# Convolution stem, forward and backward: the last chunk of the first batch's input gradient multiplied in three products, one copy per seed, middle sums added at eviction

## The chip, the cores and the metric

The kernel runs on one core of a Trainium2 chip. The metric is the device time of one execution in microseconds (us), as the median of several runs. One further execution was taken with the hardware profiler; the views of the profile and of the trace come from it.

## The reference

A strided one-dimensional convolution, a group norm with one group per channel over time, a GELU, and the gradients of all of it. In short:

```python
B, T, D, K = 2, 16000, 256, 31          # all inputs bf16
s = 2; L = (T - K) // s + 1             # 7985
h = sum(einsum('blc,cd->bld', x[:, i:i + s*L:s, :], w[i]) for i in range(K))
mu  = h.sum(1) / L;  var = ((h - mu) ** 2).sum(1) / L
out = gelu((h - mu) / sqrt(var + 1e-5) * gn_gamma + gn_beta)     # tanh form
# outputs: out, and the gradients by x, w, gn_gamma, gn_beta for a given grad_out
```

## The kernel before

**Stages.** F0 and F1 are the forward convolution of batch 0 and 1, G0 and G1 the gradient by `x` (`input_grad`), W the gradient by `w` (`weight_grad`). The GELU and its derivative for batch 1 (`gelu_batch(1, ...)`, eight units of `gelu_unit`) run beside G0 on ACT and DVE. When all eight are done, `elem_finalize(1)` forms the sums of the group norm, and `e_load`/`e_comp` can then prepare the gradient of batch 1 for each chunk.

**Order.** No instruction stands where the Python code calls it. Each call of `add` records an operation with its engine, an estimated duration, and what it reads and writes; `Plan.order` gives each a due time (from the tensor engine's progress, a slack, and the tables `lead` and `fine`, whose keys are stage, function and caller) and lists the operations engine by engine. Each engine then runs its own list in order. Transfers above 4096 bytes are issued by SP (`load` at L548, transposes by `turn` at L553) in these stages, except the stores of the transposed gradient, which POOL issues.

**Input gradient.** For each of two batches the work is four chunks `c`, two halves `pr` of a chunk, and three branches `br` in the order B, A, C. Branches and leaves come from two nested three-product splittings: instead of multiplying two weight groups by two inputs four times, one multiplies sums and differences three times. For a branch there is a middle leaf B and two outer leaves A and C. The accumulators are two pairs of PSUM banks, `px` and `pt`. One branch and half goes so:

- `g_three_b` (4 matmuls) and `g_three_ac` (8) make the middle leaf, in three products itself, in `px`. An ACT copy (L1357) carries the common product over.
- `g_seed` puts the middle leaf into `pt` as well, so that both outer leaves start from it.
- `last(A)` and `last(C)`, called while the next branch is under way, add the outer leaves into `pt` and `px`, and `g_evac` empties them: branch B into the middle sums `GRB` (ACT, `keep`, L837), branches A and C into the result tile `HO`. There is one `HO`; its store to `out_1` is issued after leaf C of branch C.

**The outer leaves, two ways.** In batch 0 an outer leaf is `g_leaf`, 16 matmuls with 512 columns (leaf A of branch A has 4 of 256). The seed is one ACT copy, `keep`, and `g_evac` adds the middle sum on DVE (L1429). In batch 1 (`GO`, `GOC`) each outer leaf is split in three products too: `g_outer` (4 matmuls, for leaf A into bank 0 and for leaf C into bank 1 of `pt`) and `g_three_ac` (8), 12 instead of 16. That needs summed weights (`w2_outer`, six additions at L688 into `W2DO` and `W2DC`) and a further moving operand for each leaf (`third`, L1283, into `GUO` and `GUC`). The seed is then longer: each outer product is written twice into a buffer `GTB`, by an ACT copy of 2048 elements for branch B (L1393) or by a DVE add of 2048 which also adds the middle sums `GRB` for branches A and C (L1397, arena<-ps,arena), and a second DVE add (L1397, ps<-ps,arena) puts middle leaf plus `GTB` into both accumulators at once. Since the middle sums are in the seed, `g_evac` in batch 1 is a plain copy on ACT (`keep`, L837, bf16).

**Memory.** `GREG` names the 28,928 bytes in which the GELU of batch 1 has its six tiles and the transposed `grad_out`, in the order h (two), y, s, y2, z, grad_out; later tenants of these bytes wait until the GELU has read them. The 8,192 bytes after it, `DNO[True]`, hold the transposed gradients of chunks 0 to 2 of batch 0 on their way out.

The tables `lead` and `fine`, some 200 numbers, are left out here.

Of the kernel before, what the change touches and what calls it, by code (L numbers as in the profile page):

```python
# [38 lines left out]
class Plan:  # L39
# [3 lines left out]
    def __init__(self, tc):  # L43
# [10 lines left out]
            "F0 f_evac last": -14.0,  # L54
            "F0 f_mm f_leaf": -265.0,
            "F0 f_mm f_outer": -52.5,
            "F0 f_mm f_three_ac": 2.5,
            "F0 f_mm f_three_b": 14.5,
            "F0 f_mm pe_turn": -455.5,
            "F0 f_outer forward": -66.5,  # L60
            "F0 f_three_b forward": 4.0,
            "F0 tt f_sums": -93.5,
            "F0 tt second": 49.5,
            "F0 tt third": 3.5,
            "F0 turn w2_part": 60.5,
            "F0 turn x_load": -50.0,
            "F0 ve f_seed": -129.5,
            "F0 ve_neg f_seed": 32.5,
            "F0 w_sub f_first": -46.5,
            "F0 zero x_load": 114.0,  # L70
            "F1 f_evac last": -156.5,
            "F1 f_mm f_leaf": -458.5,
            "F1 f_mm f_outer": 2.0,
            "F1 f_mm f_three_ac": -9.0,
            "F1 f_mm f_three_b": -31.5,
            "F1 f_outer forward": 4.0,
            "F1 f_seed forward": -37.0,
            "F1 f_three_b forward": -63.5,
            "F1 gelu_batch conv_stem_kernel": 10.5,
            "F1 gelu_unit gelu_batch": -1.5,  # L80
            "F1 load f_evac": 80.5,
            "F1 load gelu_unit": 22.0,
            "F1 load out0_store": 26.0,
            "F1 tiny elem_finalize": -56.0,
            "F1 tiny fwd_stats": -32.5,
            "F1 tt f_sums": -80.5,
            "F1 tt gelu_unit": -62.5,
            "F1 tt second": -41.0,
            "F1 tt third": -90.0,
            "F1 turn gelu_batch": 40.0,  # L90
            "F1 turn gelu_unit": -25.0,
            "F1 turn x_load": 33.0,
            "F1 ve f_seed": 8.0,
            "F1 ve_neg f_seed": -111.0,
            "F1 w_sub f_again": 35.5,
            "F1 zero f_evac": -103.0,
            "G0 cp e_comp": -6.0,
            "G0 e_comp e_load": -0.5,
            "G0 g_evac last": -13.0,
            "G0 g_mm g_leaf": -8.5,  # L100
            "G0 g_mm g_three_b": -8.0,
            "G0 g_three_b input_grad": 0.5,
            "G0 gelu_unit gelu_batch": -2.0,
            "G0 keep g_evac": -59.0,
            "G0 keep g_seed": -46.5,
            "G0 load dl_turn": 8.5,
            "G0 load e_load": 38.0,
            "G0 load g_evac": 18.0,
            "G0 load gelu_unit": 2.0,
            "G0 load load_w2": -9.0,  # L110
            "G0 spread e_comp": -1.0,
            "G0 tiny elem_finalize": -9.5,
            "G0 tt first": -52.5,
            "G0 tt gelu_unit": -0.5,
            "G0 tt third": -15.0,
            "G0 turn dl_turn": 5.0,
            "G0 turn gelu_batch": 7.5,
            "G0 w_sum load_w2": 23.0,
            "G0 zero e_comp": 10.0,
            "G1 cp e_comp": -75.5,  # L120
            "G1 e_comp e_load": 13.0,
            "G1 g_evac last": -1.5,
            "G1 g_mm g_leaf": -94.0,
            "G1 g_mm g_outer": -5.5,
            "G1 g_mm g_three_ac": -9.0,
            "G1 g_mm g_three_b": -33.0,
            "G1 g_three_b input_grad": -10.5,
            "G1 keep g_evac": 3.5,
            "G1 load dl_turn": 11.0,
            "G1 load e_load": -7.0,  # L130
            "G1 load g_evac": 15.5,
            "G1 plus g_seed": 1.5,
            "G1 spread e_comp": -6.5,
            "G1 spread g_seed": -150.0,
            "G1 tt first": -16.0,
            "G1 tt second": -15.0,
            "G1 tt third": -54.5,
            "G1 turn dl_turn": 3.5,
            "G1 w_sum w2_outer": 27.5,
            "G1 zero e_comp": -8.5,  # L140
            "W keep w_keep": -34.5,
            "W keep weight_grad": 6.0,
            "W leaf_d weight_grad": -3.0,
            "W load d_tile": -37.5,
            "W load out0_late": 105.0,
            "W load w_emit": 11.0,
            "W load weight_grad": 41.5,
            "W load x_raw": 1.5,
            "W pair_d weight_grad": -7.0,
            "W pair_x weight_grad": 0.5,  # L150
            "W turn out0_late": -77.0,
            "W ve w_done": -20.0,
            "W ve weight_grad": -19.5,
            "W w_add weight_grad": 1.0,
            "W w_add x_tile": -4.0,
            "W w_both weight_grad": 10.0,
            "W w_emit w_done": -5.0,
            "W w_emit weight_grad": -389.5,
# [310 lines left out]
def conv_stem_kernel(  # L469
# [13 lines left out]
    nc = tc.nc  # L483
# [894 lines left out]

    def g_seed(br, px, pt, outer, both):

        vx, vt = px[:], pt[:]

        def twice(v, k):
            d = [list(x) for x in v.ap]
# [513 lines left out]
```

## Time and profile before

| | us |
|---|---|
| median of 3 runs | 1165.74 |
| lowest and highest | 1163.94, 1165.88 |
| the profiled execution | 1166.96 |
| its span, first to last instruction | 1165.2 |
| mean granted clock of the tensor engine | 0.995 |

In the page, "busy" of an engine is the time in which it executed, and the number behind the bar of a group is its idle time just before the group's instructions with what ended it. A line number is that of the helper that records the operation, so a group is told by its line, its shapes and its operands: L1330 are all matmuls of the input gradient, L742 those of the forward pass, L1565 those of the weight gradient. The profiler misses some matmul records (x1880 on L1330), but not the weight loads (x1920), so matmuls are counted by weight loads. PE stands for the tensor engine, DVE for the vector engine, ACT for the scalar engine.

### The profile page before, as it was taken

The numbers are of one execution on the slowest core, as the hardware profiler recorded it, in microseconds if no ns is written. First come the engines' busy times: TensorE is split into PE (matmuls) and PEld (weight loads), VectorE is DVE, ScalarE is ACT, GpSimd is POOL, SyncE is SP. The second block draws the span as 40 slices with busy tenths as digits, with TensorE's granted clock in tenths as the row PEclk, the third lists the DMA queues.
The fourth block names the chain that finished last, engine by engine and source line by source line (L and its number), as shares of the span: only waits on it lengthen the run. The fifth ranks groups of instructions, "written<-read, shape, count | busy, mean of one in ns | idle before, by whom it ended". The sixth has DMA issues, their size and how long they took to land. (4 is left out here: it accounts for less than half of the span.)

```text
span 1165.2 us, 18856 instructions
## 1 busy us (share of the span) xinstructions
PE 1128.7 (97%) x7645; PEld 753.8 (65%) x7700; DVE 982.8 (84%) x892; ACT 553.3 (47%) x833; POOL 134.8 (12%) x221
## 2 busy tenths in 40 slices
PE   5999999999999989999899999999999999999998
PEld 3888899867777864444344444444478756666785
DVE  7997687798989997989687768777799997799995
ACT  1244454677776478788654464664332202111200
POOL 0000000000000021243232242241200000000000
PEclk8999999999999999999999999999999999999999
DMA  9476748868896598999997887676999926899367
GB/s 217 62 182 128 173 140 146 188 142 183 202 225 162 195 366 228 221 301 233 251 252 196 184 213 147 166 193 175 219 331 242 294 94 216 284 352 340 120 209 187
DMA packets 345806, 243.56 MB, mean 209 GB/s; under 512 B 233377, under 2 KB 316967, under 8 KB 341543
## 3 DMA queue, kind: packets, MB, share of 16 engines
q1 hardware_dynamic: 338615, 223.47, 73.0%
q0 software_dynamic: 7104, 18.89, 5.8%
q8 instruction: 60, 0.98, 0.4%
q14 instruction: 27, 0.22, 0.1%
HBM read 106.24 MB, written 80.25 MB: 160 GB/s over the span
## 5 line engine op out<-in xcount | busy, mean ns | idle before, releaser
L1330 PE MATMUL ps<-arena 128*128 128x512 bf16 (+1 forms) x1880 | 412.1, 377 | 13.3 <-DVE arena L1429 2.8
L742 PE MATMUL ps<-arena 128*128 128x256 bf16 (+4 forms) x3460 | 408.8, 282 | 15.7 <-DMA arena<-in_x_dram 5.7
L742 PEld LDWEIGHTS <-arena 128*128 128x128 bf16 x3460 | 338.9, 99 | 85.6 <-issue 8.6
L1330 PEld LDWEIGHTS <-arena 128*128 128x128 bf16 x1920 | 188.2, 98 | 236.0 <-issue 16.9
L1565 PE MATMUL ps<-arena 128*128 128x256 bf16 (+1 forms) x2305 | 308.6, 296 | 3.6 <-DVE arena L1635 1.9
L1565 PEld LDWEIGHTS <-arena 128*128 128x128 bf16 x2320 | 226.7, 98 | 85.6 <-DVE arena L1635 3.0
L837 ACT ACTIVATE arena<-ps 128x1024 f32<-128x1024 f32 (+1 forms) x111 | 113.0, 1022 | 242.6 <-PE ps L1565 84.1
L700 DVE TENSOR_TENSOR arena<-arena 128x2080 bf16<-128x2080 bf16 (+7 forms) x126 | 156.5, 1265 | 26.1 <-PE ps L742 25.5
L548 POOL DMA_DIRECT2D dld<-arena x144 | 105.2, 732 | 291.6 <-DMA arena<-arena 283.8
L1117 DVE TENSOR_TENSOR arena<-arena 128x2048 bf16<-128x2048 bf16 (+1 forms) x80 | 95.6, 1195 | 11.5 <-ACT arena L1109 6.0
L1533 DVE TENSOR_TENSOR arena<-arena 128x4096 bf16<-128x4096 bf16 x38 | 86.5, 2284 | 6.2 <-DMA arena<-in_x_dram 5.7
L1283 DVE TENSOR_TENSOR arena<-arena 128x1032 bf16<-128x1032 bf16 (+1 forms) x120 | 84.1, 725 | 8.3 <-PE ps L1330 5.2
L1397 DVE TENSOR_TENSOR ps<-ps,arena 128x2048 f32<-128x2048 f32 x24 | 55.1, 2297 | 25.2 <-PE ps L1330 24.4
L857 ACT ACTIVATE arena<-ps 128x512 bf16<-128x512 f32 (+1 forms) x64 | 37.1, 581 | 52.0 <-PE ps L742 50.2
L557 POOL MEMSET arena<- 128x128 bf16 (+11 forms) x40 | 9.1, 260 | 409.2 <-DVE arena L700 142.4
L1667 ACT COPY ps<-ps 128x256 f32<-128x256 f32 x54 | 19.3, 358 | 75.3 <-PE ps L1565 73.6
L1429 DVE TENSOR_TENSOR arena<-ps,arena 128x1024 bf16<-128x1024 f32 x32 | 38.8, 1218 | 12.9 <-PE ps L1330 7.6
L1397 DVE TENSOR_TENSOR arena<-ps,arena 128x2048 f32<-128x2048 f32 x16 | 36.6, 2289 | 14.5 <-ACT arena L837 10.9
L1736 DVE TENSOR_TENSOR arena<-arena 128x4608 bf16<-128x4608 bf16 x16 | 40.4, 2551 | 8.5 <-PE ps L1565 7.8
L812 ACT ACTIVATE arena<-ps 128x512 f32<-128x512 f32 x56 | 29.6, 599 | 36.8 <-PE ps L742 26.7
L1107 DVE SCALAR_TENSOR_TENSOR arena<-arena 128x2048 bf16<-128x2048 bf16 (+1 forms) x16 | 35.8, 2237 | 13.2 <-ACT arena L1104 13.2
L1232 ACT COPY arena<-arena 128x768 bf16<-128x768 bf16 (+1 forms) x64 | 36.2, 615 | 18.6 <-DVE arena L1223 14.8
(83 smaller groups left out, 772.3 us busy)
## 6 DMA issues: line engine op xcount, KB each, us to landing
arena<-in_x_dram SPq DMA_DIRECT2D x40, 1024.0 KB
dld<-arena POOLq DMA_DIRECT2D x144, 128.0 KB, 3.8
arena<-hd SPq DMA_DIRECT2D x32, 512.0 KB
out_dram<-arena SPq DMA_DIRECT2D x14, 1024.0 KB
arena<-dld SPq DMA_DIRECT2D x18, 640.0 KB
arena<-dld SPq DMA_DIRECT2D x18, 576.0 KB
vl<-arena SPq DMA_DIRECT2D x36, 256.0 KB
arena<-vl SPq DMA_DIRECT2D x9, 1024.0 KB
```

The source lines that it names most:

```text
L548: lambda: e.dma_start(out=out, in_=in_), dma=np_ * ns / 16e3 * 1.03, ns=ns, tp=SH[pk], slack=slack)
L700: lambda: nc.vector.tensor_tensor(out=o, in0=a, in1=b, op=ALU.add))
L742: yield nc.tensor.matmul(ps[:, dh, cs], lhsT=wt, rhs=mv, start=s0, stop=False, skip_group_check=True)
L837: lambda: nc.scalar.activation(out=out, in_=ps, func=ACT.Copy, scale=scale))
L1117: add("DVE", dve(nf), [o], [a, b_], lambda: V.tensor_tensor(out=o, in0=a, in1=b_, op=op))
L1283: lambda: nc.vector.tensor_tensor(out=o, in0=a, in1=b, op=ALU.subtract))
L1330: yield nc.tensor.matmul(ps[:, e, 0:wide], lhsT=lt, rhs=mv, start=s0, stop=False, skip_group_check=True)
L1397: lambda: nc.vector.tensor_tensor(out=o, in0=a, in1=b, op=ALU.add))
L1429: lambda: nc.vector.tensor_tensor(out=ho[:, :, k, :], in0=ps[:], in1=g, op=ALU.add))
L1533: add("DVE", dve(4096), [o], [a, b], lambda: nc.vector.tensor_tensor(out=o, in0=a, in1=b, op=ALU.add))
L1565: yield nc.tensor.matmul(ps[:, s, c0:c1], lhsT=lt, rhs=mv, start=s0, stop=False, skip_group_check=True)
L1736: add("DVE", dve(4608), [o], [u, v], lambda: nc.vector.tensor_tensor(out=o, in0=u, in1=v, op=ALU.subtract))
```

## The change

It has four parts and a set of new tables.

1. Chunk 3 of batch 0 is treated as batch 1 is: both outer leaves of each branch by `g_outer` and `g_three_ac`.
2. The seed of a split branch is the same for all three branches: an ACT copy of both outer products, 1024 elements, into a `GTB` of half the size, and one DVE add of 2048 which reads `px` and `GTB` twice and writes `pt` and `px`.
3. `g_evac` adds the middle sum on DVE in all chunks of both batches.
4. The six weight sums are ordered during chunk 2 of batch 0 (branch B in its first half, A and C in its second), in place of three at the beginning and three in the second half of chunk 3. `W2DO` and `W2DC` of branch B lie in the second buffer of the branch sums `GS`, those of A in the GELU's two h tiles, those of C in `DNO[True]`; `GUO` and `GUC` lie in the GELU's grad_out, y and s tiles, `GTB` in y2 and z.
5. The tables `lead` and `fine` are replaced, in all stages.

```diff
-    GTS = sb(GREG + 20992, 2, 512, dt=FP32)
-    W2DO = {MIR[br]: sb(GREG + 25088 + 4096 * i, 2, 2, 512) for i, br in enumerate(ORDER)}
-    GUO = {br: sb(94336 + 2080 * i, 2, 2, EM) for i, br in enumerate(ORDER)}
-    W2DC = {MIR[br]: sb(GREG + 4096 * i, 2, 2, 512) for i, br in enumerate(ORDER)}
-    GUC = {br: sb(o, 2, 2, EM) for br, o in zip(ORDER, (94336 + 6240, GREG + 12288, GREG + 14368))}
-    GTB = sb(GREG + 16704, 2, 2, 512, dt=FP32)
+    W2DO = {MIR[br]: sb(o, 2, 2, 512) for br, o in zip(ORDER, (94336, GREG, GREG + 28928))}
+    W2DC = {MIR[br]: sb(o, 2, 2, 512) for br, o in zip(ORDER, (98432, GREG + 4096, GREG + 33024))}
+    GUO, GUC = ({br: sb(GREG + o, 2, 2, EM) for br, o in zip(ORDER, v)} for v in ((24704, 8192, 12352), (26784, 10272, 14432)))
+    GTB = sb(GREG + 16512, 2, 512, dt=FP32)
...
-    def g_seed(br, px, pt, outer, both):
...
+    def g_seed(px, pt, outer):
+
+        if not outer:
             keep(flat2(pt), flat2(px))
+            return
+        keep(GTB.rearrange("p k f -> p (k f)"), flat2(pt))
+
+        def over(v, step, dims):
+            return bass.AP(tensor=v.tensor, offset=v.offset, ap=[list(v.ap[0]), [step, 2], *dims, [1, 512]])
+        o, i = flat2(pt), flat2(px)
+        o, x, g = over(o, i.offset - o.offset, [[512, 2]]), over(i, 0, [[512, 2]]), over(GTB, 512, [[0, 2]])
+        add("DVE", dve(2048, 1), [pt[:], px[:]], [px[:], GTB],
+            lambda: nc.vector.tensor_tensor(out=o, in0=x, in1=g, op=ALU.add))
...
-        if (b, c, br) in GO or (b, c, pr) in GOC:
-            keep(ho[:, :, k, :], ps[:])
-        else:
-            g = GRB[:, 0 if lf == A else 1]
-            add("DVE", dve(1024, 1), [ho[:, :, k, :]], [ps[:], g],
-                lambda: nc.vector.tensor_tensor(out=ho[:, :, k, :], in0=ps[:], in1=g, op=ALU.add))
+        g = GRB[:, 0 if lf == A else 1]
+        add("DVE", dve(1024, 1), [ho[:, :, k, :]], [ps[:], g],
+            lambda: nc.vector.tensor_tensor(out=ho[:, :, k, :], in0=ps[:], in1=g, op=ALU.add))
...
-    GO = {(1, c, br) for c in range(NCK) for br in ORDER} | {(0, 3, br) for br in GLAST}
...
-    GOC = {(1, c, pr) for c in range(NCK) for pr in range(2)}
...
+    GO = {(b, c) for b, c in ((0, 3), (1, 0), (1, 1), (1, 2), (1, 3))}
...
-                        both = (b, c, pr) in GOC
-                        if both:
+                        if outer:
                             if pr == 0:
                                 third(br, C_)
                             g_outer(pt, br, planes(br, C_), o, C_)
-                        g_seed(br, px, pt, outer, both)
...
+                        g_seed(px, pt, outer)
...
-        if (b, c, pr, br) == (0, 2, 1, A) and GLAST:
-            w2_outer()
+        if (b, c, pr, br) in ((0, 2, 0, C_), (0, 2, 1, C_)):
+            w2_outer(ORDER[0:1] if pr == 0 else ORDER[1:3])
         if (b, c, pr, br) == (0, 3, 0, B_):
             plan.stage = "G1"
-            if not GLAST:
-                w2_outer()
             e_load(1, 0)
...
-        if (b, c, pr, br) == (0, 3, 1, A) and GOC:
-            w2_outer(C_)
```

More of the change, by code (lines that the diff above doesn't have):

```diff
@@ L53, in __init__ @@
         self.lead = {
[L54 to L66, printed above, removed]
@@ new lines, in __init__ @@
+            "F1 f_evac last": -106.5,
+            "F1 f_mm f_leaf": -335.0,
+            "F1 f_mm f_outer": 74.0,
+            "F1 f_mm f_three_ac": -8.5,
+            "F1 f_mm f_three_b": -75.5,
+            "F1 f_three_b forward": -73.0,
+            "F1 gelu_unit gelu_batch": -2.0,
+            "F1 load gelu_unit": 23.0,
+            "F1 load out0_store": 15.0,
+            "F1 tt f_sums": -79.5,
+            "F1 tt gelu_unit": -49.5,
+            "F1 tt second": -38.0,
+            "F1 tt third": -225.5,
```

409 lines of the change are left out of this document (187 added, 222 removed).

## The prediction

> **What bounds the kernel now.** I read the head of the page first, for the engines' shares, then the busy times cut at the borders of the stages.
>
> ```profile
> span 1165.2 us, 18856 instructions
> ...
> PE 1128.7 (97%) x7645; PEld 753.8 (65%) x7700; DVE 982.8 (84%) x892; ACT 553.3 (47%) x833; POOL 134.8 (12%) x221
> ```
>
> ```profile
> 0.00:418.00 418.00, 402.42 (x3401) 333.18 (x3402) 359.53 (x350) 233.50 (x423) 7.91 (x28) 0.99 0.74 173
> 418.00:601.50 183.50, 175.50 (x833) 83.31 (x848) 154.57 (x177) 139.87 (x176) 56.04 (x79) 0.99 0.99 260
> 601.50:658.50 57.00, 56.01 (x260) 25.78 (x264) 45.70 (x67) 24.66 (x34) 14.79 (x24) 1.00 0.73 192
> 658.50:847.00 188.50, 184.09 (x844) 83.99 (x859) 141.90 (x110) 99.69 (x113) 54.08 (x87) 1.00 0.79 186
> 847.00:1165.20 318.20, 310.71 (x2316) 227.54 (x2329) 281.09 (x191) 55.55 (x90) 1.97 (x3) 1.00 0.77 244
> ```
>
> The columns are PE, PEld, DVE, ACT and POOL busy, then clock, DMA share and GB/s. The rows are forward; input gradient of batch 0, chunks 0 to 2; its chunk 3; batch 1; weight gradient. The third row is cut by count: its 264 weight loads are the 6 × 44 that chunk 3 of batch 0 issues (44 for each branch and half: 4 + 8 for the middle, 16 for each of two outer leaves). There PE is busy for 56.01 of 57.00 us, so a matmul taken out of it is worth its full time, as long as DVE, the next engine (45.70), keeps up. In the second row DVE has 154.57 of 183.50 and DMA a share of 0.99.
>
> **What a matmul is worth.** A stretch of batch 1 in which PE never pauses gives the price, one in which it does shows what a pause costs:
>
> ```profile
> 560.00:580.00 20.00, 17.11 (x71) 7.35 (x71) 0.91 1.11 233
> 760.00:780.00 20.00, 19.95 (x95) 9.14 (x95) 1.00 0.85 196
> ```
>
> In the second row 95 matmuls take 20.00 us; one or two of them are of half width, so a full one takes 0.2125 us. Chunk 3 of batch 0 today multiplies each outer leaf whole, 16 matmuls; after, 4 for the outer product and 8 for the rest. That is 4 fewer for each of 2 halves, 3 branches and 2 leaves: 48, of which 4 (leaf A of branch A) have half the width. **Term 1: 46 × 0.2125 = 9.8 us less PE.** Batch 1 does the same matmuls as before.
>
> **What DVE and ACT get.** The groups, shape by shape (count, busy us, mean ns of one, idle before and its releaser):
>
> ```profile
> L1283 DVE TENSOR_TENSOR arena<-arena 128x1032 bf16<-128x1032 bf16 x112 | 74.7, 690 | 5.6 <-PE ps L1330 5.2
> L1397 DVE TENSOR_TENSOR ps<-ps,arena 128x2048 f32<-128x2048 f32 x24 | 55.1, 2297 | 25.2 <-PE ps L1330 24.4
> L1429 DVE TENSOR_TENSOR arena<-ps,arena 128x1024 bf16<-128x1024 f32 x32 | 38.8, 1218 | 12.9 <-PE ps L1330 7.6 <-DMA out_dram<-arena 5.1
> L1397 DVE TENSOR_TENSOR arena<-ps,arena 128x2048 f32<-128x2048 f32 x16 | 36.6, 2289 | 14.5 <-ACT arena L837 10.9 <-PE ps L1330 3.3
> L837 ACT ACTIVATE arena<-ps 128x1024 f32<-128x1024 f32 x79 | 80.3, 1022 | 188.1 <-PE ps L1565 84.1 <-DVE arena L1594 51.6 <-PE ps L742 23.6
> L837 ACT ACTIVATE arena<-ps 128x1024 bf16<-128x1024 f32 x32 | 32.7, 1024 | 54.5 <-PE ps L1330 49.5 <-remote 5.0
> L837 ACT ACTIVATE ps<-ps 128x1024 f32<-128x1024 f32 x29 | 29.2, 1006 | 24.3 <-PE ps L1330 16.7 <-PE ps L1565 4.8 <-PE ps L742 2.4
> L1393 ACT COPY arena<-ps 128x2048 f32<-128x2048 f32 x8 | 14.9, 1868 | 3.2 <-PE ps L1330 3.1
> L688 DVE TENSOR_TENSOR arena<-arena 128x2048 bf16<-128x2048 bf16 x9 | 10.9, 1215 | 0.0
> ```
>
> Chunk 3 of batch 0. Each of its 6 seeds was one ACT copy from PSUM to PSUM (1.01 us); it becomes an ACT copy to the arena (1.02) and a DVE add over both accumulators (2.30), so ACT stays even and DVE gets 6 × 2.30 = 13.8. Each branch needs two more moving operands (`third`), 6 × 0.69 = 4.1. Its evictions add the middle sum on DVE today and still will. **Term 2: 17.9 us more DVE in the stretch where PE gives up 9.8.** No row shows this mix in this stretch; batch 1 (fourth stage row: DVE at 75%, PE at 98%) is the nearest.
>
> Batch 1, for each of 8 halves. Branches A and C lose one DVE add each (2 × 2.29) and four evictions move from ACT (1.02) to DVE (1.22): DVE 4.87 − 4.58 = +0.29, in all 8 × 0.29 = 2.4 us on 141.90 of 188.50, which fits. ACT loses the spread copy (1.87) and four evictions (4.10) and gets three copies (3.07): 23 us less in all, on an engine with room. What counts is the chain ahead of the leaves: a spread (1.87) or an add (2.29) and then an add (2.30) become a copy (1.02) and an add (2.30), about 1 us shorter. What PE waits for in batch 1 bounds the gain:
>
> ```profile
> PE ps L1330 <- ACT arena L837: 1.8, 4, 1.0
> PE ps L1330 <- DVE ps L1397: 1.0, 2, 0.5
> ```
>
> All idle time of PE in the stage row is 188.50 − 184.09 = 4.4 us; the evictions on ACT and the seeds on DVE carry 2.8. The evictions' wait does not go, it changes engine. **Term 3: −1.0 us**, the seeds' part; the bounds are −4.4 and, if evictions now queue behind seeds on DVE, +3 or so (one eviction of 1.22 late at some of the 24 seeds; no row shows it).
>
> **Whether DVE fits.** The stretch becomes 57.0 − 9.8 = 47.2 us, with 45.7 + 17.9 = 63.6 us of DVE work: 16.4 too much, if all of it stays there. Part can leave, and the timeline of DVE shows which:
>
> ```profile
> 590.39 1.22 DVE L688 TENSOR_TENSOR arena<-arena 128x2048 bf16<-128x2048 bf16 x1
> ...
> 597.42 2.09 DVE L1107 SCALAR_TENSOR_TENSOR arena<-arena 128x1856 bf16<-128x1856 bf16 x1 [4.07 <-ACT arena L1104]
> ...
> 610.98 1.22 DVE L688 TENSOR_TENSOR arena<-arena 128x2048 bf16<-128x2048 bf16 x1
> ...
> 613.16 1.12 DVE L1130 CUSTOM_DVE_ANT_1 arena<-arena 128x928 bf16<-128x928 bf16 x1
> ...
> 618.58 1.21 DVE L688 TENSOR_TENSOR arena<-arena 128x2048 bf16<-128x2048 bf16 x1
> ...
> 641.62 0.81 DVE L1212 TENSOR_SCALAR arena<-arena,stats 128x2048 bf16<-128x2048 bf16 x1
> ...
> 657.90 1.22 DVE L1223 TENSOR_TENSOR arena<-arena 128x2048 bf16<-128x2048 bf16 x1
> ```
>
> Six L688 sums make the weights of the outer products, five of them between 610.98 and 618.58. They are ordered during chunk 2 now, and four of the six (branches B and C) get memory that the GELU of batch 1 does not hold, so three can leave the stretch: 3.7 us. The six gradient operations between 641.62 and 657.90 (0.81, 0.75, 1.23, 0.80, 0.74, 1.22: 5.5 us) prepare chunk 1 of batch 1, which begins a whole chunk after 658.5, and can slide into batch 1, where DVE has 46 us free. Left: 16.4 − 3.7 − 5.5 = 7.2 us. The rest of the surplus must go before 601.5, where DVE has 28.9 us free, but the last GELU unit, from 597.42, starts only when ACT releases it (4.07), and its chain ends with the L1130 row at 614.28. It also holds memory: the copy buffer `GTB` of the new seed, the second outer weight of branch A and all of `GUO` and `GUC` now lie in GELU buffers. The first new seed would be wanted when its outer products are done, 52 matmuls into the stretch: 601.5 + 52 × 0.2125 = 612.5; it can begin at 614.3 and takes 1.02 + 2.30, so it is ready at 617.6. The matmuls of the next branch that do not need it (4 + 4 + 8 + 4 = 20) last 4.3 us, to 616.8; so about 1 us is lost there even if all else fits. **Term 4: half of the 7.2, 3.6 us of PE waiting**, the 1 us in it; the ends are 0 (everything leaves) and 16.4 (nothing does). I take the middle because the window already shows PE at 19.89 of 20.00 us between 600 and 620 with DVE full, which says that a full DVE is bearable for 20 us, not for 47.
>
> The replaced tables of leads reorder the other stages too, without changing their work. PE's idle time there, 418.00 − 402.42 = 15.6 and 318.20 − 310.71 = 7.5 us, bounds what that can win; what it can lose has no row. I take nothing, ±3.
>
> **The sum.** Against the profiled execution, 1166.96 us (span 1165.2 and 1.8 around it): 1166.96 − 9.8 − 1.0 + 3.6 = 1159.8. That execution lies 1.2 above the median of the three runs, 1165.74; against the median the same −7.2 gives 1158.5.
>
> **Rivals.** *All of it is kept.* The gelu tail goes early enough, DVE fits: −10.8, so 1155. For it: the idle DVE before 601.5; against it: the ACT wait at 597.42 and the DMA share of 0.99 in that stage. Chance 0.22.
>
> *DVE sets the pace of chunk 3.* If none of the 16.4 leaves, the change costs 16.4 − 10.8 = 5.6, so 1171; it decides for slower once more than 10.8 of the 16.4 stays. For it: 63.6 us of work in 47.2; against it: 9.2 has plainly somewhere to go. Chance 0.15. Between it and the forecast, 9 to 13 staying, lies no measurable change (within 0.2%, about 2.3 us, which is what a measurement of this kernel can tell): 0.08.
>
> *The store of the result holds DVE.* There is one buffer `HO`; the first eviction of a half must wait until the store of the half before has landed.
>
> ```profile
> 553.73 0.53 SPq L548 DMA_DIRECT2D out_dram<-arena  x1
> ...
> 738.45 0.52 SPq L548 DMA_DIRECT2D out_dram<-arena  x1
> ```
>
> ```profile
> 561.75 1.23 DVE L1429 TENSOR_TENSOR arena<-ps,arena 128x1024 bf16<-128x1024 f32 x1 [3.91 <-DMA out_dram<-arena]
> ```
>
> ```profile
> 563.03 3.45 PE L1330 MATMUL ps<-arena 128*128 128x512 bf16 x9 [2.83 <-DVE arena L1429]
> ```
>
> ```profile
> 749.21 1.02 ACT L837 ACTIVATE arena<-ps 128x1024 bf16<-128x1024 f32 x1 [4.50 <-remote]
> ```
>
> ```profile
> 739.73 12.55 PE L1330 MATMUL ps<-arena 128*128 128x512 bf16 x57
> ```
>
> A store takes 8.0 us to land (553.73 to 561.75), or 10.8 (738.45 to 749.21, which I read as the same wait, on ACT). From one half's last eviction to the next half's first there are 52 matmuls (the last 4 of the branch in which the eviction falls, a branch of 36, 12 of the next), 11.1 us, in batch 1 and now in chunk 3 of batch 0 too (before, 64 and 13.6). So a store that SP issues a little late is late for the eviction. On ACT that cost PE nothing (it runs through from 739.73 to 752.28); on DVE every seed and every operand behind it waits, as at 561.75, where PE lost 2.83 us and the clock fell to 0.91 in that window: 71 matmuls instead of 94, 23 × 0.2125 = 4.9 us. Two such waits among the eight halves of batch 1 and the two of chunk 3 make it −7.2 + 9.8 = +2.6, 1168, and three 1173: it decides for slower from the second on. Against it: only one of eight halves of batch 1 waited for long. Chance 0.08.
>
> The Trainium skill, "TensorE: Matmul & The Clock Gate", Part 1 (The HAM clock gate), has the clock halve only after an idle window of about 3.4 us; by that rule a wait of 2.83 us would cost 2.8 us and no more, and three late stores would be needed, not two. Here the row of 560 to 580 shows the clock already below 1 around a wait of that length, and the row decides the price that I use.
>
> *The new order elsewhere is worse* than the old by more than the saving: 7.2 + 2.3 us in stages whose work is unchanged, 1168 or more. Nothing in the profile speaks for it, the breadth of the edit does. Chance 0.07.
>
> **The numbers.** Forecast 0.40, all kept 0.22: faster 0.62. Same 0.08. Slower 0.15 + 0.08 + 0.07 = 0.30. The range reaches from 1153 (all kept and part of batch 1's 4.4 us) to 1172 (DVE sets the pace); three late stores or worse, and a gain of more than 13, are left out. Faster cases alone: 1153 to 1163.
>
> **What would show it.** Matmuls on the line of `g_mm`: 1920 weight loads become 1872. The DVE seeds (2048, into PSUM) go from 24 to 30, those into the arena from 16 to none, the evictions on DVE from 32 to 64, the operands of 1032 from 112 to 118; the ACT evictions in bf16 and the spread copies go to none. Chunk 3 of batch 0, found by its 216 or so weight loads, takes 47 to 52 us; with PE idle near the end of the GELU and DVE above 90% my term 4 is right. PE idle by 10 us or more there means that DVE sets the pace. Waits of L1429's successor for `out_dram` in batch 1, with PE waiting behind them, would be the third rival. If chunk 3 shrinks by 9 us and the total does not, the loss lies in the other stages, and the window rows say in which.

## The result, and the profile after

| | before | after |
|---|---|---|
| median, us (7 runs each, same chip) | 1163.94 | 1154.98 |
| lowest and highest | 1160.43, 1165.88 | 1153.53, 1158.27 |
| ratio with its 95% interval | | 0.9929 [0.9911, 0.9946] |
| the profiled execution, us | 1166.96 | 1154.13 |

The change makes the kernel faster by 8 to 9 us. The two profiled executions differ by 12.8, more than the medians do: the one of before lies 3.0 above its median here, the one of after 0.9 below. So the account by stages below can be wrong by some 4 us in its sum.

Busy times of after, cut at the first matmul of each chunk of the input gradient (found by counting weight loads on L1324, which was L1330). The rows are forward, chunks 0 to 3 of batch 0, chunks 0 to 3 of batch 1, weight gradient; the columns are PE, PEld, DVE, ACT, POOL, clock, DMA share, GB/s:

```profile
0.00:413.80 413.80, 401.44 (x3400) 333.07 (x3401) 359.80 (x350) 233.45 (x424) 7.94 (x28) 0.99 0.72 173
413.80:476.60 62.80, 62.18 (x326) 31.69 (x324) 56.59 (x75) 54.69 (x79) 13.69 (x22) 1.00 1.05 301
476.60:535.40 58.80, 56.76 (x266) 25.86 (x265) 55.28 (x59) 49.90 (x59) 16.64 (x32) 1.00 1.01 269
535.40:591.60 56.20, 56.20 (x265) 25.84 (x264) 53.65 (x62) 39.69 (x44) 15.37 (x23) 1.00 0.91 244
591.60:638.40 46.80, 46.71 (x218) 21.14 (x216) 43.66 (x53) 17.58 (x24) 16.26 (x26) 1.00 0.77 181
638.40:690.00 51.60, 48.21 (x217) 21.45 (x216) 39.49 (x39) 22.11 (x30) 13.81 (x23) 0.97 0.81 190
690.00:736.90 46.90, 46.70 (x218) 21.17 (x217) 38.25 (x37) 30.89 (x38) 13.91 (x25) 1.00 0.90 217
736.90:783.50 46.60, 46.42 (x218) 21.18 (x217) 36.98 (x36) 17.70 (x22) 15.66 (x27) 1.00 0.78 189
783.50:832.20 48.70, 48.30 (x233) 22.58 (x232) 34.95 (x27) 12.85 (x15) 11.58 (x16) 1.00 0.85 224
832.20:1152.40 320.20, 309.61 (x2307) 225.96 (x2305) 279.25 (x191) 53.84 (x88) 0.52 (x1) 0.99 0.74 235
```

The same cuts in before, for the four stages that moved most (chunks 2 and 3 of batch 0, chunk 0 of batch 1, weight gradient):

```profile
540.40:602.20 61.80, 57.73 (x261) 26.23 (x265) 47.32 (x52) 40.88 (x45) 16.41 (x24) 0.97 1.06 257
602.20:659.20 57.00, 56.01 (x260) 25.77 (x264) 45.70 (x67) 24.41 (x35) 14.79 (x24) 1.00 0.73 192
659.20:707.10 47.90, 46.37 (x212) 21.12 (x216) 35.27 (x27) 29.88 (x37) 16.95 (x26) 1.00 0.80 186
850.70:1165.20 314.50, 307.06 (x2292) 225.17 (x2305) 277.48 (x189) 54.52 (x89) 0.52 (x1) 1.00 0.76 242
```

Chunk 3 of batch 0 went from 57.0 to 46.8 us, and in these 46.8 PE is busy for 46.71: nothing waits. DVE, which I had given 17.9 us more there, has 2.0 less (43.66 for 45.70). Chunk 2 lost 5.6 us, the forward pass 4.1. Against that, chunk 0 of batch 1 is 3.7 longer and the weight gradient 5.7.

The operations themselves are those counted ahead. Groups of after, shape by shape (count, busy us, mean ns, idle before):

```profile
L1324 PEld LDWEIGHTS <-arena 128*128 128x128 bf16 x1872 | 183.5, 98 | 226.8 <-issue 11.4 <-DVE arena L1277 3.9
L1277 DVE TENSOR_TENSOR arena<-arena 128x1032 bf16<-128x1032 bf16 x118 | 78.2, 691 | 4.2 <-issue 2.3 <-ACT arena L1226 0.9 <-PE ps L1324 0.6
L1395 DVE TENSOR_TENSOR arena<-ps,arena 128x1024 bf16<-128x1024 f32 x64 | 77.0, 1218 | 8.1 <-PE ps L1324 4.8 <-ACT arena L1226 2.2 <-issue 0.8
L1385 DVE TENSOR_TENSOR ps<-ps,arena 128x2048 f32<-128x2048 f32 x30 | 68.9, 2296 | 26.0 <-ACT arena L831 14.8 <-PE ps L1324 11.1
```

1872 weight loads, 118 operands, 64 evictions, 30 seeds. L1395 (evictions) and L1385 (seeds) together take 145.9 us; in before L1397 and L1429 took 55.1 + 36.6 + 38.8 = 130.5. The 15.4 more, and six operands, are real DVE work; it was done elsewhere than in chunk 3. Where, the timeline of DVE in chunk 2 shows, with the first and the last instruction of the last GELU unit:

```profile
574.59 2.08 DVE L1101 SCALAR_TENSOR_TENSOR arena<-arena 128x1856 bf16<-128x1856 bf16 x1
...
588.21 1.12 DVE L1124 CUSTOM_DVE_ANT_1 arena<-arena 128x928 bf16<-128x928 bf16 x1
```

In before the same two stood at 597.42, behind a wait of 4.07 us for ACT, and 613.16. The unit now starts without a wait and is over at 589.3, ahead of chunk 3. Measured from the start of chunk 3 that is 12.2 us earlier (17.0 ahead of it instead of 4.8). DVE does 56.59 + 55.28 + 53.65 = 165.5 us in chunks 0 to 2, for 155.4 in before at the same cuts, although they are 6.5 us shorter.

Two new waits are seen. In chunk 0 of batch 1, the timelines of PE, DVE and SP:

```profile
658.54 41.72 PE L1324 MATMUL ps<-arena 128*128 128x512 bf16 x184 [3.39 <-DVE arena L1277]
```

```profile
653.17 0.75 DVE L1208 TENSOR_SCALAR arena<-arena,stats 128x2048 bf16<-128x2048 bf16 x1 [1.48 <-DMA arena<-dyd]
655.81 0.81 DVE L1206 TENSOR_SCALAR arena<-arena,stats 128x2048 bf16<-128x2048 bf16 x1 [1.88 <-DMA arena<-hd]
```

```profile
626.91 16.64 SPq L549 DMA_TRANSPOSE arena<-arena  x6
643.65 0.50 SPq L544 DMA_DIRECT2D out_dram<-arena  x1
644.20 0.35 SPq L544 DMA_DIRECT2D arena<-dyd  x1
644.59 1.81 SPq L544 DMA_DIRECT2D arena<-hd  x1
```

Read from the end: PE waits 3.39 us for an operand (L1277). That stands on DVE behind two gradient operations (`e_comp`) that wait for their loads; SP issued these loads only after six transposes, which held its queue for 16.64 us. PE's 48.21 us of work where other chunks have 46.4 to 46.7, at a clock of 0.97, is the rest of the stage's loss. In the weight gradient a wait of the same kind stands at 1009 (PE, DVE, SP), there for loads from `dld` that SP issued behind five loads of the input:

```profile
1009.48 5.77 PE L1528 MATMUL ps<-arena 128*128 128x256 bf16 x36 [2.80 <-DVE arena L1598]
```

```profile
1003.54 4.62 DVE L1496 TENSOR_TENSOR arena<-arena 128x4096 bf16<-128x4096 bf16 x2 [3.23 <-DMA arena<-dld]
```

```profile
974.72 20.30 SPq L544 DMA_DIRECT2D arena<-in_x_dram  x5
995.07 4.30 SPq L544 DMA_DIRECT2D arena<-dld  x4
```

### The profile page after: what moved, and what is told of

It reads as the page before. It is cut to its first block, busy times and chain, and to the rows that moved or that the text cites. A ratio compares the mean times of both kernels' runs of the same rounds, so it can differ in the third digit from the quotient of the medians.

```text
span 1152.4 us, 18848 instructions
## 1 busy us (share of the span) xinstructions
PE 1122.5 (97%) x7652; PEld 749.9 (65%) x7652; DVE 997.9 (87%) x920; ACT 532.7 (46%) x817; POOL 125.4 (11%) x221
## 5 line engine op out<-in xcount | busy, mean ns | idle before, releaser
L736 PE MATMUL ps<-arena 128*128 128x256 bf16 (+4 forms) x3460 | 407.8, 281 | 12.4 <-DMA arena<-in_x_dram 5.5
L1324 PE MATMUL ps<-arena 128*128 128x512 bf16 x1872 | 404.5, 377 | 6.9 <-DVE arena L1277 3.4
L1324 PEld LDWEIGHTS <-arena 128*128 128x128 bf16 x1872 | 183.5, 98 | 226.8 <-issue 11.4
L831 ACT ACTIVATE arena<-ps 128x1024 f32<-128x1024 f32 x109 | 111.0, 1022 | 262.3 <-PE ps L1528 90.1
L694 DVE TENSOR_TENSOR arena<-arena 128x2080 bf16<-128x2080 bf16 (+8 forms) x126 | 156.5, 1267 | 34.0 <-PE ps L736 33.6
L544 POOL DMA_DIRECT2D dld<-arena x144 | 104.3, 727 | 261.9 <-DMA arena<-arena 248.3
L1277 DVE TENSOR_TENSOR arena<-arena 128x1032 bf16<-128x1032 bf16 (+1 forms) x126 | 87.5, 725 | 8.7 <-ACT arena L1226 3.3
L1385 DVE TENSOR_TENSOR ps<-ps,arena 128x2048 f32<-128x2048 f32 x30 | 68.9, 2296 | 26.0 <-ACT arena L831 14.8
L1395 DVE TENSOR_TENSOR arena<-ps,arena 128x1024 bf16<-128x1024 f32 x64 | 77.0, 1218 | 8.1 <-PE ps L1324 4.8
L1351 ACT COPY ps<-ps 128x512 f32<-128x512 f32 x48 | 27.7, 578 | 46.8 <-PE ps L1324 45.6
L772 ACT ACTIVATE ps<-ps 128x256 f32<-128x256 f32 x75 | 27.6, 369 | 34.7 <-PE ps L736 33.5
L1614 DVE TENSOR_TENSOR arena<-arena 128x2048 bf16<-128x2048 bf16 x36 | 42.8, 1218 | 0.8 <-DMA out_dram<-arena 0.8
```

The lines of the kernel that those rows point to most:

```text
L544: lambda: e.dma_start(out=out, in_=in_), dma=np_ * ns / 16e3 * 1.03, ns=ns, tp=SH[pk], slack=slack)
L694: lambda: nc.vector.tensor_tensor(out=o, in0=a, in1=b, op=ALU.add))
L736: yield nc.tensor.matmul(ps[:, dh, cs], lhsT=wt, rhs=mv, start=s0, stop=False, skip_group_check=True)
L831: lambda: nc.scalar.activation(out=out, in_=ps, func=ACT.Copy, scale=scale))
L1277: lambda: nc.vector.tensor_tensor(out=o, in0=a, in1=b, op=ALU.subtract))
L1324: yield nc.tensor.matmul(ps[:, e, 0:wide], lhsT=lt, rhs=mv, start=s0, stop=False, skip_group_check=True)
```

## The experiments

Stage times of all kernels, cut in the same way from one profiled execution each (us), and the ratio of the runs to before with its interval. The first four kernels have before's order; the next seven have after's, the last two of these but for the loads that they move; the three at the end have an order of their own.

| kernel | forward | b0: c0 to c2 | b0: c3 | b1: c0 | b1: c1 to c3 | W | ratio |
|---|---|---|---|---|---|---|---|
| before | 417.9 | 184.3 | 57.0 | 47.9 | 143.6 | 314.5 | 1 |
| `b_pe48` | 416.6 | 183.7 | 54.4 | 49.7 | 143.5 | 312.0 | 1.0003 [0.9985, 1.0021] |
| `b_pe48dve` | 416.3 | 184.7 | 67.5 | 48.9 | 143.5 | 312.9 | 1.0101 [1.0082, 1.012] |
| `b_newseed` | 416.3 | 185.7 | 56.1 | 50.3 | 159.3 | 314.7 | 1.0162 [1.0145, 1.0179] |
| after | 413.8 | 177.8 | 46.8 | 51.6 | 142.2 | 320.2 | 0.9929 [0.9911, 0.9946] |
| `a0` | 414.0 | 181.5 | 46.4 | 51.3 | 141.9 | 318.3 | 0.9921 [0.9901, 0.994] |
| `x_pe48` | 414.6 | 181.3 | 55.0 | 49.8 | 142.2 | 316.8 | 0.9979 [0.9963, 0.9995] |
| `x_dve` | 413.6 | 178.2 | 59.9 | 53.3 | 141.8 | 320.6 | 1.0037 [1.0024, 1.005] |
| `x_oldseed` | 413.6 | 178.5 | 46.4 | 53.2 | 160.5 | 315.3 | 1.0053 [1.0038, 1.0067] |
| `x_eload` | 414.8 | 179.5 | 46.4 | 47.5 | 141.9 | 322.9 | 0.9877 [0.9856, 0.9898] |
| `x_two` | 414.1 | 178.5 | 46.4 | 46.5 | 142.2 | 328.2 | 0.9945 [0.9926, 0.9964] |
| `e_nosplit` | 414.9 | 191.9 | 56.1 | 56.0 | 148.1 | 329.6 | 1.0278 [1.0255, 1.03] |
| `e_newtab` | 412.8 | 192.5 | 56.2 | 58.8 | 167.1 | 325.9 | 1.039 [1.037, 1.0411] |
| `e_oldtab` | 442.8 | 195.0 | 60.3 | 67.3 | 153.1 | 342.9 | 1.0823 [1.0799, 1.0848] |

**After once more, on the chip of the next runs (`a0`).** No edit.

> The changed kernel once more, beside the kernel before on the same chip and profiled again: how far the stage times of one execution differ from another's. Both theories: ratio 0.992 to 0.994 to the kernel before. If the 5.8 us that the weight gradient gave back and the 3.8 us of chunk 0 of batch 1 belong to the order of the work, they are there again within 1 us; if they are chance, at least one of them moves by more than 2 us.

1155.3, ratio 0.9921: the gain repeats. Each stage repeats within 2 us, but for chunks 0 to 2, which take 3.7 us more. What the weight gradient gives back moved by 1.9 us, from 5.7 to 3.8, which lies between the two marks that were set for it.

**One part of the change without the other: the tables and the split.** `e_oldtab` is after with before's `lead` and `fine`, `e_newtab` is before with after's. `e_nosplit` is after with chunk 3 of batch 0 multiplied whole:

```diff
-    GO = {(b, c) for b, c in ((0, 3), (1, 0), (1, 1), (1, 2), (1, 3))}
+    GO = {(b, c) for b, c in ((1, 0), (1, 1), (1, 2), (1, 3))}
```

> The changed kernel with the old tables of leads, so with the order that they give. Theory O (the order pays: the new tables finish the GELU of batch 1 about 25 us earlier and so clear DVE for chunk 3): the GELU ends after the start of chunk 3 as it did before, DVE sets the pace there, chunk 3 takes 52 to 60 us instead of 46.7, and the total is 5 us or more above the changed kernel, near the kernel before (ratio to before 0.997 to 1.005). Theory M (the matmuls pay, whatever the order): chunk 3 takes 47 to 49 us and the ratio to before stays at 0.991 to 0.995.

> The kernel before with the new tables, its work unchanged: what the order alone does. Theory O: the GELU ends earlier here too, but chunk 3 has its 264 matmuls and takes 56 to 57 us; the time is within 0.3% of before, or worse, since the tables were made for other work. If the tables bring the gain by themselves (a rival to the split), the ratio is 0.992 to 0.996.

> The changed kernel without part 1: chunk 3 of batch 0 multiplies its outer leaves whole again, seeds and evictions of batch 1 and the tables as changed. By term 1 chunk 3 takes 9.8 us longer (56 to 57 us) and the total is 8 to 11 us above the changed kernel, so level with the kernel before (ratio 0.999 to 1.002). If the gain came from the seeds of batch 1 or the tables, it is less than 4 us above the changed kernel.

1260.59, 1210.71 and 1195.9 us. Before is some 46 us slower with after's tables than with its own, and after 105 us slower with before's: some five and twelve times what the change brings. `e_nosplit` gives chunk 3 as it should: 56.1, so 9.7 more than in `a0`. But it loses 10 in chunks 0 to 2, 11 in batch 1 and 11 in the weight gradient, where it does nothing new: the due times no longer fit, and every engine's list is another.

`e_oldtab` has the whole split in before's tables. Its last GELU unit is over on DVE at 636.2, 1.5 us ahead of chunk 3, and DVE does as little there as in after, but the chunk takes 60.3 us:

```profile
637.70:698.10 60.40, 51.66 (x213) 22.27 (x217) 44.26 (x55) 17.31 (x24) 13.78 (x23) 0.92 0.61 155
```

PE's two longest waits in it, 2.04 and 3.45 us, end with the new seed, and that had waited for an ACT copy. So a GELU that is over before chunk 3 is not enough by itself.

No part of this change can be priced by taking it out of the source. The following runs keep the lists of after, or of before, in their order and change what single entries do.

**The price of the 48 matmuls in after's order (`x_pe48`).** Each `g_outer` of chunk 3 is issued twice, the second time over the first result: 48 matmuls more.

```diff
+            for e, wide, lt, mv, s0 in more:
+                yield nc.tensor.matmul(ps[:, e, 0:wide], lhsT=lt, rhs=mv, start=s0, stop=False, skip_group_check=True)
```

> The changed kernel, its order held, with every outer product of chunk 3 of batch 0 multiplied twice (12 times 4 matmuls of 512 more, the result the same): the matmuls that the split saves, put back, with no other work changed. 48 x 0.2125 = 10.2 us. If PE sets the pace in chunk 3 (both theories, for this order), chunk 3 takes 56 to 57 us and the total is 9 to 11 us above the changed kernel. If DVE set it, less than 5.

Chunk 3, the window row:

```profile
595.90:650.90 55.00, 55.00 (x257) 25.06 (x256) 43.52 (x51) 17.55 (x24) 15.95 (x26) 1.00 0.59 151
```

Its chunk 3 is 8.6 longer (8 of the 48 extra matmuls are issued before the border of the stage), and PE is busy for all of 55.00 us: in after's order the matmuls are worth their full time there. The total rose by 5.9 us (6.7 by the ratios), less than the 10.2 that they take: chunk 0 of batch 1 (49.8) and the weight gradient (316.8) are each 1.5 shorter than in `a0`. That is not because the loads came in better time: in chunk 0 of batch 1 PE waits 3.25 us behind them, and 3.30 in `a0`. But in `a0` three waits (1.86 us in chunks 0 to 2, this one, and 1.58 in the weight gradient) are each followed by 3.41 us at half clock, 1.7 us lost, and in these stages of `x_pe48` none is (last section). So of what chunk 3 gains, this run does not show how much is given back behind it. With the matmuls put back the time is still 2.5 us below before (ratio 0.9979): a smaller part of the gain does not come from them.

**How full DVE is in chunk 3 (`x_dve`).** Two more adds of 1024 behind each of the six seeds, 12 × 1.22 = 14.6 us.

```diff
+            for _ in range(2 if more else 0):
+                yield nc.vector.tensor_tensor(out=gs, in0=gt, in1=gt, op=ALU.add)
```

> The changed kernel, its order held, with two more DVE adds of 1024 fp32 behind each of the 6 seeds of chunk 3 (12 x 1.22 = 14.6 us of DVE whose result nobody reads). DVE has 46.7 - 43.6 = 3.1 us free in chunk 3. Theory O (DVE was cleared just enough): PE must wait, chunk 3 grows by 8 us or more and the total by 6 to 12. Theory M (DVE's surplus slides into the next chunks, where it is idle a quarter of the time): the total grows by less than 4.

```profile
591.90:651.80 59.90, 49.45 (x218) 21.41 (x216) 57.51 (x65) 17.69 (x24) 16.30 (x26) 0.97 0.56 141
```

1168.9: the chunk takes 13.5 us more, almost all that was added, with DVE at 57.51 of 59.90. So DVE has no more than about 3 us of room in chunk 3 of after (46.80 − 43.66): the fear that it would fill up there was right, only much of its other work had gone elsewhere.

**The matmuls left out of before, in before's order (`b_pe48`), and the same with 17.9 us of DVE work more (`b_pe48dve`).** Two matmuls of each outer half-leaf are skipped in chunk 3, in the first; in the second each seed of chunk 3 is an ACT copy and a DVE add of 2048, and the operands of two more products are computed. The gradient by `x` of that chunk lacks the products left out.

```diff
-            for e, wide, lt, mv, s0 in jobs:
+            for n, (e, wide, lt, mv, s0) in enumerate(jobs):
+                if n in less:
+                    continue
```

> The kernel before, its order held, without 4 of the 16 matmuls of each outer leaf of chunk 3, batch 0 (48 left out, so the gradient by x lacks their products): the relief of PE alone, nothing added on DVE. Term 1: chunk 3 takes 46.8 to 48 us instead of 57.0 and the total is 8 to 10 us below the kernel before. If the weight gradient cannot start earlier without waiting (it was 314.5 us long in the kernel before, 318 to 323 in the changed one), it grows by 2 to 5 us here too and the total falls by only 5 to 8.

> The same, its order held, with the DVE work of the split added: a DVE add of 2048 behind each of the 6 seeds of chunk 3 and six operands of 1032 more (17.9 us; their values are not the split's). Here the GELU of batch 1 still ends 12 us into chunk 3. This is term 4 by itself: the prediction says 3.6 us above the run without the DVE work, within 0 and 16.4. Theory O (with the old order DVE sets the pace of chunk 3): 7 us or more, so that nothing is left of the gain. Theory M: less than 3.

`b_pe48`: 1164.56 against 1165.26 of before on that chip, no difference; the profiled execution is 2.9 below that median, so that the 2.6 us which chunk 3 lost in it can't be told from nothing. Its chunk 3 (window row; the timeline of PE; of DVE the last of the GELU, the last weight sum and the operand that PE's second wait ends with):

```profile
600.30:654.70 54.40, 47.29 (x218) 20.93 (x217) 43.82 (x65) 23.29 (x34) 13.56 (x24) 1.00 0.71 199
```

```profile
612.19 4.69 PE L1332 MATMUL ps<-arena 128*128 128x512 bf16 x22 [1.16 <-ACT arena L837]
619.33 6.87 PE L1332 MATMUL ps<-arena 128*128 128x512 bf16 x30 [2.44 <-DVE arena L1283]
626.41 10.95 PE L1332 MATMUL ps<-arena 128*128 128x512 bf16 x50 [0.22 <-ACT ps L1359]
638.74 8.80 PE L1332 MATMUL ps<-arena 128*128 128x512 bf16 x42 [1.37 <-ACT arena L837]
```

```profile
611.27 1.12 DVE L1130 CUSTOM_DVE_ANT_1 arena<-arena 128x928 bf16<-128x928 bf16 x1
...
616.70 1.22 DVE L688 TENSOR_TENSOR arena<-arena 128x2048 bf16<-128x2048 bf16 x1
...
618.58 0.69 DVE L1283 TENSOR_TENSOR arena<-arena 128x1032 bf16<-128x1032 bf16 x1
```

PE's own work fell to 47.29 us, and 7.1 us of waiting came in its place. Half of it is early in the chunk: at 611 PE has done 52 matmuls and stands for ACT, at 617 for an operand, while DVE works off the GELU, its sums and the weights. With the new DVE work on top (`b_pe48dve`) the chunk takes 67.5 us:

```profile
601.00:668.50 67.50, 52.20 (x217) 22.14 (x216) 59.54 (x75) 23.10 (x34) 13.66 (x24) 0.90 0.57 160
```

1176.59, by the ratio 12 us slower than before. So nearly the same change of work in chunk 3 goes with a chunk 10.2 us shorter in after's order and 10.5 us longer in before's. What differs between the two is the order that surrounds it, the buffers, and the weight sums, five of which still stand in the chunk here.

**The new seeds and evictions of batch 1 alone.** `b_newseed` puts them into before's lists, `x_oldseed` puts the old ones into after's. In both the middle sums of batch 1 are not always the ones that the reference adds, so its gradient by `x` is another; the instructions are of the kind and size that is meant.

```diff
+            if not old:
+                return nc.scalar.activation(out=gf, in_=pf, func=ACT.Copy, scale=1.0)
+            if br == B_:
+                return nc.scalar.copy(out=GTB2, in_=p)
+            return nc.vector.tensor_tensor(out=GTB2, in0=p, in1=GRB, op=ALU.add)
...
+            lambda: nc.vector.tensor_tensor(out=ho[:, :, k, :], in0=ps[:], in1=g, op=ALU.add) if b == 0 else
+            nc.scalar.activation(out=ho[:, :, k, :], in_=ps[:], func=ACT.Copy, scale=1.0))
```

This is `x_oldseed`; `b_newseed` is its mirror image, with the new copy and add in the places of the old ones and the eviction on DVE.

> The changed kernel, its order held, with the seeds and evictions of batch 1 as they were (ACT spread or DVE add into a double GTB, plain ACT evictions): parts 2 and 3 undone in batch 1 alone. Term 3 of the prediction: 1.0 us slower, within 0 and 4.4. If the new seeds carry the gain (a rival), 5 us or more slower.

> The kernel before, its order held, with the seeds and evictions of batch 1 as the change has them (ACT copy of 1024, one DVE add, middle sums added at eviction on DVE): parts 2 and 3 alone in batch 1. Term 3: 1.0 us faster, within -4.4 and +3. A gain above 4.4 would mean that PE waited for the seeds in ways that its waits do not show.

Both are slower than their base, by about the same: batch 1 takes 209.6 instead of 191.5 in `b_newseed` and 213.7 instead of 193.2 in `x_oldseed`. An exchange of the seeds that is dear in both directions prices the misfit between lists and durations, not the seeds. These two runs settle nothing about term 3; it is left to the comparison of before and after, each in its own order.

**The late loads of batch 1 (`x_eload`).** The first two loads for chunk 1 of batch 1 are taken ahead of the six transposes, all else in after's order:

```diff
+        up = [i for i in order if self.ops[i]["kind"] == "G1 load e_load" and self.ops[i]["part"] == 0][:2]
+        at = [i for i in order if self.ops[i]["kind"] == "G1 turn dl_turn" and self.ops[i]["part"] == 0][0]
+        order = [i for i in order if i not in up]
+        k = order.index(at)
+        order = order[:k] + up + order[k:]
```

> The changed kernel with one move in the list: the two loads for the first half of the gradient of chunk 1, batch 1, go ahead of the six transposes that SP issues before them. If the 3.8 us that chunk 0 of batch 1 gave back are DVE waiting for these loads with PE's operands queued behind, chunk 0 takes 47 to 48.5 us instead of 51.5 and the total falls by 2 to 5 us. If the wait was for something else, nothing changes (within 1.5 us).

SP's timeline (L552 and L557 are L544 and L549 of after) and the row of chunk 0 of batch 1:

```profile
626.79 0.32 SPq L552 DMA_DIRECT2D arena<-dyd  x1
627.16 1.28 SPq L552 DMA_DIRECT2D arena<-hd  x1
628.72 16.88 SPq L557 DMA_TRANSPOSE arena<-arena  x6
```

```profile
640.70:688.20 47.50, 46.63 (x218) 20.99 (x217) 39.15 (x38) 21.98 (x30) 13.80 (x23) 1.00 0.84 187
```

The chunk takes 47.5 instead of 51.3 in `a0`, the clock stays at 1.00, and the total is 1149.31 against `a0`'s 1155.3 (6.0 us, 5.1 by the ratios): it beats both kernels. (Its profiled execution, 1154.78, was the longest of its five, so the 322.9 of its weight gradient in the table is rather too high.) That the late loads caused the loss in chunk 0 of batch 1 is shown.

**The same for the weight gradient (`x_two`).** `x_eload` with the four loads from `dld` that after's trace has at 995.07 moved ahead of the five loads of the input. In the edit, `dl` lists these four by their numbers, and 2979 is the first of the five.

```diff
+        dl = [2986, 2985, 2988, 2987]
...
+        order = [i for i in order if i not in dl]
+        k = order.index(2979)
+        order = order[:k] + dl + order[k:]
```

> The kernel after with both moves in SP's queue: the two loads that chunk 1 of batch 1 needs go ahead of six transposes, as in x_eload, and in the weight gradient four loads of the gradient from dld, which SP issues behind five loads of the input (973.33 to 994.57 in x_eload's trace), go ahead of these five. Theory Q (the weight gradient is longer after than before because these loads come late: in x_eload's trace DVE waits 3.10 us for dld, PE behind it 1.04 and 2.30, and in the two 20 us windows around it the clock is 0.95 and 0.88, which costs 40 x 0.085 = 3.4 more): the waits at 1005 and 1009 go and the weight gradient, 322.9 there, comes to 316 to 318; the total falls by 3 to 6 us from x_eload's 1149.3. Theory S (the loads only change places: the loads of the input come 4 us later and the next operand is late instead): weight gradient 321 to 325, total 1147 to 1152, with new PE waits between 985 and 1030.

1157.25, ratio 0.9945: 8 us are lost again, and the weight gradient (328.2) is longer than either expectation had it. The timelines of SP, DVE and PE, and a window:

```profile
973.85 2.23 SPq L559 DMA_DIRECT2D arena<-dld  x4
976.12 38.55 SPq L559 DMA_DIRECT2D arena<-in_x_dram  x11
```

```profile
992.06 2.29 DVE L1511 TENSOR_TENSOR arena<-arena 128x4096 bf16<-128x4096 bf16 x1 [7.74 <-DMA arena<-in_x_dram]
...
1005.91 4.62 DVE L1511 TENSOR_TENSOR arena<-arena 128x4096 bf16<-128x4096 bf16 x2 [2.94 <-DMA arena<-in_x_dram]
```

```profile
1011.85 140.00 PE L1543 MATMUL ps<-arena 128*128 128x256 bf16 x997 [7.63 <-DVE arena L1613]
```

```profile
1007.70:1027.70 20.00, 15.80 (x106) 11.85 (x108) 15.79 (x12) 2.14 (x6) 0.00 (x0) 0.76 0.75 241
```

DVE now waits 7.74 and then 2.94 us for the input, PE for DVE 7.63, and in the 20 us from the middle of PE's wait on the clock is 0.76. The loads only changed places, and the input was needed first. So the wait for `dld` in after's weight gradient isn't an order of two groups on SP that could be turned round; chunk 0 of batch 1, at 46.5, shows once more what the first move does.

## Why the prediction was right, and where it was not

The forecast was 1158.5 with a range of 1153 to 1172, and faster with a chance of 0.62. Measured are 1154.98; by the ratio, 8.3 us of gain for the 7.2 of the sum. The direction and the total came out, but of the four terms the second had the wrong place and the fourth did not come. That the total lies so near is luck: by the two profiles the forward pass and chunks 0 to 2 gained 4.1 + 6.5 us and chunk 0 of batch 1 and the weight gradient lost 3.7 + 5.7, none of which is in the sum, and the 3.6 of waiting was not there.

- **Term 1, −9.8 for 48 matmuls: right.** Chunk 3 lost 10.2, `e_nosplit` lost the gain in that chunk again (9.7), and in `x_pe48` PE is busy for all of its longer chunk.
- **Term 2, 17.9 us more DVE: right as work, wrong as a place.** The counts and durations are as foretold. But the stretch holds 43.66 us of DVE, not 45.70 + 17.9; nearly 20 us left it, where I had found room for 3.7 + 5.5. The groups of the two stretches say what left: the GELU's last operations (7.8 us in before, none in after), six of the twelve that prepare batch 1's gradient (5.5, as forecast), two of five weight sums (2.5, for 3.7), and some 5 us of operands (16 of 1032 elements stand there, where 17 + 6 were to be expected).
- **Term 3, −1.0: not contradicted.** Chunks 1 to 3 of batch 1 went from 143.6 to 142.2. No experiment isolates it.
- **Term 4, +3.6 of waiting: this step failed.** I held that the GELU's last unit could not start before 597.42, because it waited for ACT there, and that its chain therefore ended at 614.28. That was taken from the old order. In the new one the unit starts 22.8 us earlier, and DVE does some 10 us more in chunks 0 to 2, out of chunk 3's way; PE waits for 0.1 us in chunk 3. Of the rivals, "all of it is kept" described chunk 3 as it came, and its 1155 is the time. I had set its chance at 0.22 against 0.40, on the strength of that wait and of the DMA share of 0.99 there. The mechanism of term 4 itself is real: in before's order PE loses 7.1 us without any new DVE work, half of it while DVE is at the GELU, its sums and the weights, and with the new work the chunk is 10.5 us longer, DVE busy for 59.54 of 67.50. That is the nearest to "DVE sets the pace". The edit with before's tables (`e_oldtab`) has a longer chunk too, but with DVE busy for 44.26 of 60.40: what PE waits for there are seeds behind an ACT copy.
- **Other stages "nothing, ±3": the size was wrong.** Over four traces in before's order and seven in after's, chunk 3 begins at 600.3 to 602.2 and at 591.6 to 595.9, some 8 us earlier. Of this I had only bounded the forward part (15.6 us of idle time, now 12.4). Behind chunk 3, chunk 0 of batch 1 lost 3.7 (after) and 3.4 (`a0`), the weight gradient 5.7 and 3.8. Neither was foreseen as a place. The first is a pair of loads behind transposes, shown by `x_eload`; I had looked at HO's store and at memory, not at what else the new order puts into SP's queue.
- **The rival of the store** did not come: no L1395 waits for `out_dram` in batch 1 with PE behind it. Its count of three late stores at 2.8 us each is one short: −7.2 + 8.5 = +1.3 lies within the 2.3 us that the prediction calls no change. **The new order worse elsewhere** came in two stages and was outweighed in two others.

Two things stay open. Which entry of the tables lets the GELU finish earlier was not tried alone, and `e_oldtab` shows that its early end does not suffice; which other entries matter is not known. And the weight gradient is 3.8 to 5.7 us longer in after's order than in before's, in `a0` and `after`, although its work is the same. The rows say of what: from before to after PE idles 3.2 us more there (10.59 for 7.44) and is busy for 2.6 more (309.61 for 307.06), 1.7 of which is the half clock behind the wait of 2.80 us. `x_pe48` (316.8) idles 9.04 us and has no such stretch, `x_dve` (320.6) idles 10.60 and has one. Late loads are what the wait at 1009 ends with; the one at 866 (1.57 us) ends with DVE's own work. `x_two` rules out the simple exchange of two groups, and why the loads come late was not settled.

## What to carry to other kernels

A cut in the bounding engine's work is worth what the other engines' queues allow at that place: with 48 matmuls fewer the chunk was 10 us shorter in after's order, and the time of before's order, where DVE still had the GELU and five weight sums in that chunk, did not change. When a schedule is written out for certain durations, test a part of a change with the order of the instructions held fixed; taken out of the source, it measured the misfit (+41 to +105 us) instead. After a stage has become shorter, look in the queue that issues the transfers for loads that now stand behind slow entries: moving two loads ahead of six transposes gave 5 to 6 us more.

## What the runs showed of the hardware that was not expected

A wait of PE can cost more than itself, even a short one. In chunk 0 of batch 1 a wait of 3.39 us came with a clock of 0.97 over the stage and 48.21 us of matmuls where 46.4 to 46.7 are usual, so some 1.6 us on top; without the wait, in `x_eload`, the clock is 1.00 and PE has 46.63. Around the wait of 2.80 us in after's weight gradient:

```profile
992.20:1012.20 20.00, 17.20 (x117) 11.71 (x116) 16.64 (x9) 4.53 (x6) 0.00 (x0) 0.95 0.96 325
1012.20:1032.20 20.00, 20.00 (x129) 12.75 (x128) 16.18 (x11) 1.72 (x5) 0.00 (x0) 0.97 0.89 278
```

The clock of 0.95 and 0.97 is another 20 × 0.08 = 1.6 us. Cut finer, the loss behind both waits is one stretch of 3.41 us at a clock of 0.50 (658.53 to 661.94, and 1010.11 to 1013.52), so 1.7 us, the same for 3.39 us of waiting and for 2.80. The length alone does not tell whether it comes: behind 1.58 us of waiting in `a0` it does,

```profile
869.65:873.06 3.41, 3.22 (x16) 2.29 (x17) 3.41 (x4) 0.36 (x2) 0.00 (x0) 0.50 0.51 143
```

and behind 3.25 in `x_pe48` and 2.60 in `b_pe48` it does not. The stretches lie on a grid: those two of after begin 351.58 us apart, 103 × 3.4134, and those of `a0` (528.32, 661.44, 869.65) 39 and 61 steps of 3.413 apart. Counted by these steps in all fourteen traces, but for the first 30 us and the last steps, every step at full clock in which PE idles for 1.98 us or more is followed by a step at 0.50, and none with 1.81 or less; between the two both are seen. The 1.58 us of `a0` fall into one step with 0.34 of the wait behind them (1.92); the 3.25 of `x_pe48` are cut by a border at 669.54 into 1.89 and 1.36. So by these traces a wait of 2 to 3.4 us costs 1.7 us more where it falls inside one step, and may cost nothing more where a border cuts it. The Trainium skill, "TensorE: Matmul & The Clock Gate", Part 1, lets the clock halve only after an idle window of about 3.4 us; the wait of 3.39 can be read so, the ones of 2.80 and 1.58 can't, and the rows decide. The other surprise is the price of transposes on a queue: six held SP for 16.64 us, 2.8 each (20.34 in `x_pe48`), and a load that would have taken 0.3 to issue stood behind all of them.
